# Engine orders held as tables in place of a list scheduler, in a fused attention and MLP kernel

## The chip, the cores and the metric

The kernel runs on one core of a Trainium2 chip. The metric is the device time of one execution in microseconds (us). Three runs of the kernel before gave a median of 744.11 us, from 744.04 to 744.46. The profile comes from one further execution.

## What is computed

The reference takes one batch of S = 2048 rows of D = 512 bfloat16 numbers. It normalises each row, and adds to the input an attention branch and an MLP branch that both read the normalised rows:

```python
def _A_ref(x, wq, wk, wv, wo):          # H = 32 heads of Dh = 16, one K and one V for all
    q = (x @ wq) by heads
    k, v = x @ wk, x @ wv
    scores = q k^T * Dh ** -0.5
    o = softmax(scores) @ v
    return o by rows @ wo
def _B_ref(x, w1, b1, w2, b2):          # F = 1792
    return gelu(x @ w1 + b1) @ w2 + b2
xn = _layernorm(x)
return x + _A_ref(xn, ...) + _B_ref(xn, ...)
```

## The kernel before

**Tiles.** The queries are cut into 4 blocks of 512 and the 32 heads into 8 groups of 4, which gives 32 pairs of block and group. For each pair the scores of 4 heads against 16 blocks of 128 keys are made as tiles of 128 keys by 512 queries: 64 tiles per pair, 2048 in all. Three tiles make a unit `u`; there are 683 units. Units use two sets of three PSUM banks in turn, so the scores of unit `u+2` overwrite those of unit `u`.

**A unit.** TensorE makes its three score tiles (L1055, one matmul each). A string in the code, `DTAB`, says which of the three go to VectorE; the others go to ScalarE. ScalarE takes the exponential of its one to three tiles in a single instruction (L1078, buffer `E`). For its tiles VectorE makes the exponential by integer arithmetic on the bits of a bfloat16: an add and clamp that reads PSUM and writes `Dt` (L1109, called the clamp below), and then, for a batch of tiles together, three steps that add constants and so make four shifted copies (L1156 on VectorE, called the posts; one of the three steps, an addition in place on one tile at a time, stands in L1152 and goes either to GpSimd or to VectorE). TensorE multiplies each `E` tile and each copy in `Dt` by a (scaled) V and adds them up in one PSUM bank, 32 of its 128 partitions for each of the four heads (L1122, called PV below). So an `E` tile costs one PV and a VectorE tile five.

**Side work.** Between these stand, on TensorE, the matmuls of the MLP and of the projections (L724, four at a time on 32 columns each, bank 7) and their evacuations on VectorE (L1221, L1249, L1301). At the end of each pair VectorE copies the sums out (L1168), DMAs re-lay them, and GpSimd or VectorE divides by the softmax sums (L1201). ScalarE computes the GELU of the MLP in two bursts, after units 182 and 512 (L1262). Some matmuls on zeros (L1419, L1420, L1422) fill gaps on TensorE.

**The end.** The last group's sums are normalised without DMAs: two shuffles on VectorE (L1209), for each half of 256 queries a logarithm (L1211) and an exponential (L1212) on ScalarE, two multiplies on VectorE (L1214); then the last output matmuls (`wol`, L724), three adds on VectorE (L1410), one copy on ScalarE (L1413), and the stores.

**What waits for what.** A score group waits until ScalarE and VectorE have read the banks that it overwrites: the exponential and the clamps of two units before. An exponential waits for its scores. A clamp waits for its scores and a free `Dt` slot; a PV waits for its exponential, post or GpSimd step. Every engine is given its own list of instructions and works through it in that order, so whatever stands in front of a waiting instruction decides when it is reached.

**What sets the order.** The kernel is recorded as a list of operations with reads and writes (`Prog.add`). Before emission a list scheduler (`Prog.schedule`, `Prog.pick_pe`) plays the program through with modelled durations: at each step it takes the engine that is free first, and of its ready operations the one with the earliest due time (ready time plus an allowance of its kind, or a number from the table `PRO_DUE` for the prologue). TensorE takes scores first; a clamp has an allowance of -20, so it goes ahead of posts (+1). A GpSimd step is started together with a VectorE instruction of at least 0.4 modelled us that is not `lock`ed (posts and some others are), and waits for a `gate`, the VectorE instruction before it. Where TensorE is expected idle the scheduler puts in matmuls on zeros. `Prog.emit` then turns dependences into semaphore waits and leaves out those that an earlier wait on the same engine already covers.

Of the kernel before, what the change touches and what calls it, by code (L numbers as in the profile page):

```python
# [10 lines left out]
P = 128  # L11
# [11 lines left out]
WIN = 3.413  # L23
HAM_T = 0.35
HAM_PHASE = 1.5

FILL_GAP = 0.25
FILL_U = 0.8
FILL_FROM = 30.0
PV_MIN = 2  # L30
PV_S = 1
P1_ALLOW = -20.0
EV_ALLOW = -2.0
S_WAIT = 0.1
P_WAIT = 0.0
# [3 lines left out]
PL_GATE = 0.1  # L39
PL_WIN = 0.4  # L40
PL_TAKE = 1.0
PL_DUE = 3.0
PL_START = 0.065
PL_SEM = 0.16
PL_FREE = 0.06
NE_ND_KB = (23, 19, 11, 6)
LA = 34
LB = 120
LY = 5
LP = 121  # L50
LS = 122
FIN_G = 2
FIN_F = 0
LAL = 30.0
LCO = 0.0
PRO_FROM = 2.0
GAP_BANK = 2
TBL = 1
# [5 lines left out]
Y_ALLOW = 2.0  # L64
H_ALLOW = 1.0
YT_ALLOW = (3,3,3,3)
WF_ALLOW = 1.5
QP_ALLOW = 1.5
# [11 lines left out]
EARLY = {23: 2}  # L80
FG = 7
UB2 = 2
YS = 19
HA = 58
HB = 168
Q_DUE = 16.0
# [14 lines left out]
PRO_DUE = (0,0,0,0,0,0,0,0,0,0,0,0.4,0.5,0.6,0.7,1017.1,901.894,890.936,0,911.47,982.75,1039.3,992.512,983.425,908.277,857.795,1021.4,984.567,1036.75,779.535,923.986,886.19,884.173,908.812,866.914,834.53,725.116,986.245,833.576,894.096,955.163,1016.7,841.68,1010.86,972.641,1071.46,918.455,991.63,996.77,917.66,1009.78,888.843,894.798,974.195,844.378,976.646,989.53,1004.34,861.884,890.838,860.34,962.694,933.585,834.453,733.954,908.291,843.106,1011.73,842.736,890.595,888.932,972.911,996.819,1013.78,960.534,901.05,840.158,948.36,842.524,854.02,1001.52,730.495,963.942,849.46,720.905,847.543,1027.14,854.874,859.03,995.253,996.641,1000.03,875.182,940.656,1013.08,927.264,901.825,865.47,856.153,1017.36,898.923,721.588,947.112,923.899,849.462,1031.22,1030.72,955.02,950.514,841.636,863.865,1004.42,992.309,974.33,882.517,1063.14,878.579,949.38,1005.69,1003.02,817.428,985.366,903.631,841.221,906.182,996.735,900.069,852.002,852.002,852.002,852.002,1009.23,962.572,984.69,1005.83,885.252,884.008,917.146,1057.84,908.105,1006.45,929.851,817.484,1057.79,1057.79,928.858,847.552,883.135,883.135,883.135,883.135,922.749,923.172,934.91,721.558,720.974,893.495,886.877,974.293,964.313,954.793,978.549,983.34,928.83,865.239,917.084,866.847,962.244,1027.57,864.398,920.685,923.146,941.861,844.389,901.982,1022.62,984.525,886.906,964.025,844.452,949.617,849.009,875.152,818.81,901.963,856.265,854.212,961.178,901.027,865.835,840.629,957.632,1025.29,1025.29,1025.29,1025.29,1025.29,1025.29,1025.29,949.479,1004.42,860.932,881.214,848.587,848.972,947.715,861.854,861.854,908.371,861.95,830.564,1013.59,920.851,852.231,848.667,834.623,834.623,873.394,849.031,984.612,984.612,983.72,865.867,901.395,857.833,1017.64,1052.68,991.698,950.486,1018.53,908.301,863.879,988.505,933.383,888.733,852.632,852.632,852.632,852.632,852.632,852.632,1001.37,972.862,921.214,1021.48,1021.48,1021.48,1021.48,1021.48,887.495,1015.8,875.099,1001.3,870.169,921.11,993.696,925.73,1005.52,961.579,848.728,1006.32,1008.12,876.619,942.093,990.844,990.844,990.844,990.844,994.103,987.859,1014.2,1014.2,1014.2,1012.8,1014.2,1014.2,1014.2,1014.2,860.884,855.696,855.696,844.754,855.696,855.252,855.696,895.571,985.973,1012.46,980.32,856.139,865.908,864.432,863.808,1004.31,985.998,788.801,903.822,865.794,984.664,894.041,1009.69,982.782,877.356,890.884,901.51,1027.88,899.618,997.552,997.552,963.952,935.705,935.705,962.628,989.577,926.43,865.864,863.945,853.609,967.557,837.03,1014.88,859.692,1006.82,1030.15,992.552,999.391,861.643,1009.24,857.784,829.305,826.367,None,None,None,None,None,920.941,None)  # L101
KV_ORD = (1, 2, 3, 4, 0)
KV_DVE = ()
DU = dict(sd=50.88, sa=19.13, ag=-17.19, ln=-33.66, xn=14.6, xa=-30.73, tr=-23.53, eva=22.21, evd=14.86, k=23.66, kt=26.82, km=39.07, v=-7.76, q=15.28, vf=17.24, v0=29.19, qt0=9.89)
# [8 lines left out]

class _Op:
    __slots__ = ("eng", "fn", "deps", "sdeps", "stream", "amt", "need", "ticket", "waits", "clock", "occ", "lat",
                 "allow", "kind", "tag", "nun", "outs", "rel", "lock", "pm", "rdy", "start", "end", "vis", "idx", "done", "due", "real", "docc")


class Prog:
# [5 lines left out]
    def __init__(self, nc):  # L125
        self.nc = nc
        self.ops = []
        self.writer = {}
        self.readers = {}
        self.accs = {}  # L130
        self.chain = {}
        self.in_chain = True
        self.filler = None
        self.pro_filler = None
        self.fill_gap = None
        self.fill_deps = []
        self.early = []
        self.log = []

    def add(self, eng, fn, r=(), w=(), acc=None, dma=None, occ=0.1, lat=0.15, allow=1.0, kind=None, tag=None, after=(), due=None, lock=False, docc=0.0):  # L140
        if len(self.ops) < len(PRO_DUE):
            due = PRO_DUE[len(self.ops)]
# [7 lines left out]
        op.occ, op.lat, op.allow, op.kind, op.tag = occ, lat, allow, kind, tag  # L150
        op.idx = len(self.ops)
        op.done = False
        op.due = due
        op.rel = None
        op.pm = any(k == ("bank", 7) or k[0] == ("bank", 7) for k in w)
        deps, sdeps = {}, {}

        def dep(o, raw):
            if o is None or o is op:
                return  # L160
            if o.stream == eng == "pe":
                sdeps.setdefault(id(o), (o, False))
                return
            deps[id(o)] = o
            sdeps[id(o)] = (o, True)
# [26 lines left out]
        for o in after:  # L192
            sdeps.setdefault(id(o), (o, True))
        if self.in_chain:
            o = self.chain.get(eng)
            if o is not None:
                sdeps.setdefault(id(o), (o, False))
            self.chain[eng] = op
        op.sdeps = list(sdeps.values())
# [3 lines left out]
    @staticmethod  # L203
    def due(o):
        return (o.rdy + o.allow if o.due is None else o.due), o.idx

    def pick_pe(self, t, cand, allr, mode, visit, cgbusy):
        S = [o for o in cand if o.kind == "S"]
        rest = [o for o in cand if o.kind != "S"]
        nxt = min([o.rdy for o in allr if o.kind == "S"] + [t + 9.0])  # L210
        if mode == "col":
            end = max(cgbusy)
            if t < end - 0.01:
                if t < end - 0.216 + 0.03:
                    c = [o for o in rest if o.tag is not None and cgbusy[o.tag[1]] <= t]
# [12 lines left out]
        if S:  # L228
            return S[0]
# [1231 lines left out]
```

## Time and profile before

| | before |
|---|---|
| median of 3 runs | 744.11 us (744.04 to 744.46) |
| the profiled execution: its own time | 744.43 us |
| its span, first to last instruction | 742.7 us |
| TensorE matmul busy (modelled ends) | 727.6 us, 9030 matmuls |
| VectorE busy | 730.4 us, 1411 instructions |
| ScalarE busy | 730.9 us, 744 instructions |
| GpSimd busy | 382.9 us, 548 instructions |
| granted TensorE clock | 1.00 |

Between the span and the time of that execution lie 1.73 us outside the first and last instruction, and that execution was 0.32 us over the median. In the page, PE is TensorE's matmuls, PEld its weight loads, DVE VectorE, ACT ScalarE, POOL GpSimd, SP the queue that issues DMAs. Busy is the union of an engine's recorded instructions; records of neighbours can overlap, since an instruction is recorded as started while the one before it still drains. Idle before an instruction is put down to whoever released it last.

### The profile page before, as it was taken

To read this page: it belongs to the slowest core of one execution; us is meant where nothing else is said; L and a number is where in the kernel's file an instruction comes from. 1 tells how busy PE (TensorE), PEld (TensorE's weight loads), DVE (VectorE), ACT (ScalarE), POOL (GpSimd) and SP (SyncE) were. 2 spreads that over 40 slices of the span, in tenths; PEclk is the share of its full clock that TensorE was granted. 3 is DMA by queue.
4 is the path that set the end of the run, shared out by engine and by line. 5 is a ranking of instruction groups with operands and counts; after the bars stand their busy time and mean duration, and the time that the engine had idled before them with its cause. 6 is when DMAs were issued, how large, how long until landed. Compare 5 with 4: busy or idle time off the path is not lost.

```text
span 742.7 us, 22080 instructions
## 1 busy us (share of the span) xinstructions
PE 727.6 (98%) x9030; PEld 212.4 (29%) x9030; DVE 730.4 (98%) x1411; ACT 730.9 (98%) x744; POOL 382.9 (52%) x548
## 2 busy tenths in 40 slices
PE   7999999999999999999999999999998999999998
PEld 4322222222233222222222222222232222222222
DVE  8999999999999999999999999999999999999996
ACT  8899999999999999999999999999999999999997
POOL 7444555554533546545656455343644656555561
PEclk9999999999999999999999999999999999999999
DMA  9200100000010010100101010100100101010011
GB/s 304 74 19 17 30 11 17 24 11 16 15 46 24 18 37 18 24 16 14 27 13 28 25 39 16 35 20 11 23 17 23 29 20 38 16 37 26 10 30 38
DMA packets 31198, 23.34 MB, mean 31 GB/s; under 512 B 16385, under 2 KB 25722, under 8 KB 31098
## 3 DMA queue, kind: packets, MB, share of 16 engines
q1 hardware_dynamic: 30954, 21.80, 11.1%
q8 instruction: 72, 1.18, 0.7%
q14 instruction: 28, 0.23, 0.1%
q10 hardware_dynamic: 144, 0.13, 0.1%
HBM read 13.08 MB, written 2.35 MB: 21 GB/s over the span
## 4 chain that ended last, share of the span: by engine, by line
ACT 70%; PE 19%; DVE 8%; DMA 1%; SPq 1%; issue 0%; DVEq 0%
ACT E L1078 70%; PE pAll L1122 8%; PE pAll L1055 6%; PE pAll L724 4%; DVE Dt L1109 4%; DVE Dt L1156 3%; DMA b1row<-in_B_b_dram 1%; SPq L731 1%; DVE Of L1168 0%; PE pAll L718 0%; PE pAll L1422 0%; DVE x_sb L1249 0%; DVE xnT L877 0%; DVE ub L1410 0%; DVE qp L1221 0%
## 5 line engine op out<-in xcount | busy, mean ns | idle before, releaser
L1078 ACT ACTIVATE E<-pAll 128x1024 bf16<-128x1024 f32 (+1 forms) x676 | 680.5, 1282 | 0.7 <-PE pAll L1055 0.5
L1152 POOL TENSOR_SCALAR Dt<-Dt 128x512 int16<-128x512 int16 x454 | 342.2, 754 | 325.5 <-DVE Dt L1156 112.6
L1122 PE MATMUL pAll<-Dt,V 128*32 128x512 bf16 x2775 | 408.2, 383 | 2.4 <-DVE Dt L1156 1.3
L1109 DVE TENSOR_SCALAR Dt<-pAll 128x512 int16<-128x512 f32 (+1 forms) x541 | 369.8, 698 | 1.4 <-PE pAll L1055 0.3
L1122 PE MATMUL pAll<-E,V 128*32 128x512 bf16 x1493 | 303.6, 383 | 0.2 <-DVE Of L1168 0.2
L1156 DVE TENSOR_SCALAR Dt<-Dt 128x1024 int16<-128x1024 int16 (+6 forms) x540 | 290.1, 564 | 0.4
L1055 PE MATMUL pAll<-QT,KT 32*128 32x512 bf16 x2048 | 267.1, 384 | 4.6 <-ACT E L1078 2.4
L1055 PEld LDWEIGHTS pAll<-QT,KT 32*128 32x128 bf16 x2048 | 66.6, 90 | 295.4 <-ACT E L1078 282.3
L1122 PEld LDWEIGHTS pAll<-Dt,V 128*32 128x32 bf16 x2775 | 102.6, 95 | 102.7 <-issue 68.0
L1122 PEld LDWEIGHTS pAll<-E,V 128*32 128x32 bf16 x1493 | 72.7, 94 | 44.0 <-issue 33.1
L724 PE MATMUL pAll<-xnT,w_sb 128*32 128x512 bf16 x896 | 84.8, 383 | 0.0
L724 PE MATMUL pAll<-w_sb,x_sb 128*32 128x512 bf16 x448 | 76.6, 384 | 0.0
L724 PE MATMUL pAll<-w_sb,ub 128*32 128x512 bf16 x448 | 64.3, 383 | 0.1
L724 PE MATMUL pAll<-wop,oTp 128*32 128x512 bf16 x256 | 51.2, 382 | 0.0
L1201 POOL TENSOR_TENSOR oTp<-OfP,rbP 128x256 bf16<-128x256 f32 (+1 forms) x28 | 22.5, 809 | 14.5 <-DVE Dt L1156 7.9
L724 PEld LDWEIGHTS pAll<-xnT,w_sb 128*32 128x32 bf16 x896 | 21.4, 95 | 26.7 <-issue 16.8
L724 PE MATMUL pAll<-xnT,wq_sb 128*32 128x512 bf16 x256 | 26.8, 383 | 0.0
L1152 DVE TENSOR_SCALAR Dt<-Dt 128x512 int16<-128x512 int16 x101 | 26.6, 286 | 0.0
L1168 DVE COPY Of<-pAll 128x512 f32<-128x512 f32 x31 | 21.2, 685 | 0.1
L1249 DVE TENSOR_SCALAR x_sb<-pAll,b1T 128x512 bf16<-128x512 f32 x28 | 20.8, 744 | 0.0
L1249 DVE TENSOR_SCALAR ub<-pAll,b1T 128x512 bf16<-128x512 f32 x28 | 20.8, 743 | 0.0
L724 PEld LDWEIGHTS pAll<-w_sb,x_sb 128*32 128x32 bf16 x448 | 18.4, 95 | 8.1 <-issue 6.6
(121 smaller groups left out, 260.8 us busy)
## 6 DMA issues: line engine op xcount, KB each, us to landing
OfP<-Of SPq DMA_DIRECT2D x124, 32.0 KB, 2.0
rbP<-rden_rows SPq DMA_DIRECT2D x124, 32.0 KB, 1.8
w_sb<-in_B_w_dram SPq DMA_DIRECT2D x2, 1792.0 KB, 11.3
x_sb<-in_A_x_dram SPq DMA_DIRECT2D x18, 128.0 KB, 2.3
QT<-qp SPq DMA_DIRECT2D x124, 16.0 KB, 1.8
x_sb<-in_A_x_dram SPq DMA_DIRECT2D x7, 256.0 KB, 4.4
out_dram<-x_sb SPq DMA_DIRECT2D x12, 128.0 KB, 1.9
wq_sb<-in_A_wq_dram SPq DMA_DIRECT2D x1, 512.0 KB, 5.8
```

Source lines behind the costliest of these rows:

```text
L724: add("pe", lambda e, c=c, j=j: e.matmul(o[c, :], l[:, c], rh, start=start, stop=stop, tile_position=(0, 32 * j)), r, [(k, j) for k in w] ...
L731: return add(eng, lambda e: e.dma_start(o, i), r, w, dma=stream, occ=occ, lat=lat, allow=allow, **kw)
L1055: ins = e.matmul(o, l, rh, start=True, stop=True, tile_position=(q0, 0))
L1078: o = act(lambda e: e.activation(E[:, s0:s0 + na, :], bank(b0, na).rearrange("p (a n) -> p a n", a=na), ACT.Exp, scale=LN2 / 128.0), w=[B( ...
L1109: op = dve(lambda e: e.tensor_scalar(Dt[:, s:s + n, :], bank(bk, n).rearrange("p (a n) -> p a n", a=n), float(127 * 128) + SPL_D, SPL_MIN, ...
L1122: add("pe", lambda e, a, b: e.matmul(pO[32 * j:32 * j + 32, :], V1[:, v, kt, :], rhs, start=a, stop=b, tile_position=(0, 32 * j)), r=r + [ ...
L1152: add("pool", lambda e, d=d, k=k: e.tensor_scalar(d, d, 1.0, float(k), ALU.mult, ALU.add), [], [(("D", base[o > 0] + q), o)], occ=PL_OCC, ...
L1156: dve(lambda e, d=view(o, nb), q=view(i, nb), k=k: e.tensor_scalar(d, q, float(k), None, ALU.add), r=keys(i), w=keys(o), n=nb * n * TBW, m ...
L1168: op = dve(lambda e: e.tensor_copy(Of[:, i, :], pO), w=["O", ("Of", i)], allow=0.0)
L1201: "pool", lambda e, c=c: e.tensor_tensor(oTp[0:n, sl, c], OfP[0:n, s, c], rbP[0:n, s, c], ALU.mult),
L1249: dve(lambda e: e.tensor_scalar(ubs[tb % 2][:, ft, :], pM, b1T[:, ft:ft + 1], None, ALU.add), r=["b1T"], w=M4 + [ukey(tb, ft)], n=TBW + 57 ...
```

## The change

The scheduler with its allowances, `PRO_DUE` and the rules for fillers is taken out. In its place stand tables: `ORD`, for each engine a string of two-character numbers that says how far each operation moves from its place in the recorded list; `GATE`, for each GpSimd step either that VectorE does it, or which operation it waits for besides its data, or none; and `FILLS`, the places and waits of the 154 matmuls on zeros. `Prog.arrange` reads them. The operations, their engines (101 of the L1152 steps stay on VectorE), the tiles, buffers, `DTAB` and `Prog.emit` stay as they were, so the same instructions run; only their order on an engine, the gates of GpSimd, and with them which semaphore waits are left, can differ.

```diff
-    def pick_pe(self, t, cand, allr, mode, visit, cgbusy):
...
-    def schedule(self):
...
+FILLS = ((0, 'p', 0, (18, 28)),
...
+         (5800, 'O', 2, (18,)),
+         (5804, 'O', 0, (18,)))
...
+def numbers(s):
+    n = len(ABC)
+    at = {c: i for i, c in enumerate(ABC)}
+    return [at[a] * n + at[b] - n * n // 2 for a, b in zip(s[::2], s[1::2])]
...
+    def arrange(self):
         ops = self.ops
+        for o, g in zip([o for o in ops if o.kind == "pl"], numbers(GATE), strict=True):
+            if g == ON_DVE:
+                o.eng = o.stream = "dve"
+                o.kind, o.occ, o.lat = "post", o.docc, D_LAT
+            elif g:
+                o.deps.append(ops[o.idx + g])
+                ops[o.idx + g].need = True
+        seq = {}
+        for e, _ in self.SECTIONS:
+            own = [o for o in ops if o.eng == e]
+            seq[e] = [own[i + d] for i, d in enumerate(numbers(ORD[e]))]
+            assert len({o.idx for o in seq[e]}) == len(own) == len(seq[e])
+        for p, kind, cg, ids in FILLS:
...
+            seq["pe"].insert(p, f)
...
+        while any(at[e] < len(seq[e]) for e in seq):
+            n = len(out)
+            for e in seq:
+                while at[e] < len(seq[e]) and all(id(o) in done for o in seq[e][at[e]].deps):
+                    out.append(seq[e][at[e]])
+                    done.add(id(out[-1]))
+                    at[e] += 1
+            assert len(out) > n
...
-        pr.schedule()
+        pr.arrange()
```

What the tables do to the orders, engine by engine: SyncE's 508 entries stand as before, so every DMA is issued in the old order. On ScalarE two neighbours of 733 change places. On VectorE 1409 entries stand in both orders, and 1003 of them can be kept in one common sequence; on GpSimd 400 of 544; on TensorE 2391 of 7511 (fillers left out). Up to the first score groups, at 23.5 us of the trace, all five engines have the old order with the old waits.

**Place 1: VectorE, the stretch that ran from 75.6 to 80.4 us.** L1109 (after: L936) are clamps, L1156 (L982) posts, L1249 (L1073) the evacuation of an MLP matmul, L1182 (L1006) a reciprocal of softmax sums. Before:

```order
L1156 TENSOR_SCALAR Dt<-Dt 128x2x1536
L1109 TENSOR_SCALAR Dt<-pAll 128x512 x2
L1249 TENSOR_SCALAR ub<-pAll,b1T 128x512
L1109 TENSOR_SCALAR Dt<-pAll 128x512
L1182 RECIPROCAL den<-den 128x32
L1156 TENSOR_SCALAR Dt<-Dt 128x1536
L1156 TENSOR_SCALAR Dt<-Dt 128x512
L1109 TENSOR_SCALAR Dt<-pAll 128x512
```

After, the same place:

```order
L982 TENSOR_SCALAR Dt<-Dt 128x2x1536
L936 TENSOR_SCALAR Dt<-pAll 128x512 x2
L1073 TENSOR_SCALAR ub<-pAll,b1T 128x512
L982 TENSOR_SCALAR Dt<-Dt 128x1536
L1006 RECIPROCAL den<-den 128x32
L936 TENSOR_SCALAR Dt<-pAll 128x512
L982 TENSOR_SCALAR Dt<-Dt 128x512
L982 TENSOR_SCALAR Dt<-Dt 128x2x1536
```

The clamp after the evacuation has moved behind the post of 1536 columns and the reciprocal. Place 1 is one of many of this kind: 241 clamps have more VectorE work ahead of them than before, 72 less, 228 the same.

**Place 2: TensorE after the second GELU burst, the stretch that ran from 566.5 to 571.4 us.** L1055 (L884) are score groups, L1122 (L949) PVs, L1422 (L1234) matmuls on zeros, L718 (L554) sums of squares of the queries. Before:

```order
L1422 MATMUL pAll<-xnT,zeros 32x512 x4
L1122 MATMUL pAll<-Dt,V 32x512 x19
L1055 MATMUL pAll<-QT,KT 128x512 x3
L718 MATMUL pAll<-sqq,sel 32x512
L1122 MATMUL pAll<-E,V 32x512
L718 MATMUL pAll<-sqq,sel 32x512
L1122 MATMUL pAll<-Dt,V 32x512 x3
L1122 MATMUL pAll<-E,V 32x512
L1122 MATMUL pAll<-Dt,V 32x512 x3
L1055 MATMUL pAll<-QT,KT 128x512 x3
```

After:

```order
L949 MATMUL pAll<-Dt,V 32x512 x2
L554 MATMUL pAll<-sqq,sel 32x512
L1234 MATMUL pAll<-xnT,zeros 32x512
L949 MATMUL pAll<-Dt,V 32x512 x5
L884 MATMUL pAll<-QT,KT 128x512 x3
L949 MATMUL pAll<-Dt,V 32x512
L949 MATMUL pAll<-E,V 32x512
L949 MATMUL pAll<-Dt,V 32x512 x5
L884 MATMUL pAll<-QT,KT 128x512 x3
```

Both sums of squares now stand ahead of the first score group shown. The run of 19 PVs in front of that group is broken up: among those that have moved behind it are the PVs of the two latest posts that the run waited for, and the later of these two posts has itself moved behind six instructions that followed it on VectorE, two clamps among them.

**Place 3: the end of ScalarE's program.** L1078 (L906) is the last exponential of the scores, L1211 (L1035) the logarithm and L1212 (L1036) the exponential of the last normalisation, one instruction for each half of the queries. Before:

```order
L1078 ACTIVATE E<-pAll 128x1536
L1078 ACTIVATE E<-pAll 128x1024
L1211 ACTIVATE rbP<-rbP 128x256 x2
L1212 ACTIVATE rbP<-rbP,lnb 128x256 x2
L1413 ACTIVATE ub<-pAll 128x512
```

After:

```order
L906 ACTIVATE E<-pAll 128x1536
L906 ACTIVATE E<-pAll 128x1024
L1035 ACTIVATE rbP<-rbP 128x256
L1036 ACTIVATE rbP<-rbP,lnb 128x256
L1035 ACTIVATE rbP<-rbP 128x256
L1036 ACTIVATE rbP<-rbP,lnb 128x256
L1228 ACTIVATE ub<-pAll 128x512
```

The first half's exponential has moved ahead of the second half's logarithm; nothing else moves on ScalarE.

More of the change, by code (lines that the diff above doesn't have):

```diff
@@ L111, in vcost @@
     return n / 0.96e3 / mode + 0.065
+def numbers(s):
+    n = len(ABC)
+    at = {c: i for i, c in enumerate(ABC)}
+    return [at[a] * n + at[b] - n * n // 2 for a, b in zip(s[::2], s[1::2])]
 class _Op:
-    __slots__ = ("eng", "fn", "deps", "sdeps", "stream", "amt", "need", "ticket", "waits", "clock", "occ", "lat",
-                 "allow", "kind", "tag", "nun", "outs", "rel", "lock", "pm", "rdy", "start", "end", "vis", "idx", "done", "due", "real", "docc")
+    __slots__ = ("eng", "fn", "deps", "odeps", "stream", "amt", "need", "ticket", "waits", "clock", "occ", "lat", "kind", "tag", "lock", "idx", "real", "docc")
 class Prog:
@@ L130, in __init__, with add @@
         self.accs = {}
[L131 to L142, printed above, removed]
+        self.fillers = {}
+    def add(self, eng, fn, r=(), w=(), acc=None, dma=None, occ=0.1, lat=0.15, kind=None, tag=None, lock=False, docc=0.0):
         op = _Op()
@@ L149, in add @@
         op.ticket = None
-        op.occ, op.lat, op.allow, op.kind, op.tag = occ, lat, allow, kind, tag
+        op.occ, op.lat, op.kind, op.tag = occ, lat, kind, tag
         op.idx = len(self.ops)
[L152 to L156, printed above, removed]
+        deps, odeps = {}, {}
         def dep(o, raw):
@@ L191, in add @@
             self.accs.setdefault(acc, []).append(op)
[L192 to L199, printed above, removed]
+        op.odeps = list(odeps.values())
         self.ops.append(op)
         return op
-    @staticmethod
-    def due(o):
-        return (o.rdy + o.allow if o.due is None else o.due), o.idx
@@ L1056, in fn @@
                 return ins
-            return add("pe", fn, r, [B(3 * x + i) for i in range(len(ts))], occ=0.216, lat=S_LAT, allow=-1.0, kind="S")
+            return add("pe", fn, r, [B(3 * x + i) for i in range(len(ts))], occ=0.216, lat=S_LAT, kind="S")
         eptr = [0]
@@ L1110, in p1 @@
                                                  float(127 * 128) + SPL_D, SPL_MIN, ALU.add, ALU.max),
[L1111 removed]
+                       w=[B(b) for _, b in ds] + [(("D", s + i), 0) for i in range(n)], n=n * TBW, kind="p1")
             for i, (t, _) in enumerate(ds):
```

661 lines of the change are left out of this document (160 added, 501 removed), and 151 rows, old and new, of the table FILLS.

## The prediction

> **What bounds the kernel now.** I looked first at the span, then at busy time by stretch, then at what each group of instructions waited for, and last at the tail.
>
> ```profile
> span 742.7 us, 22080 instructions
> ```
>
> The view of busy time by stretch, for ScalarE alone, from the first exponential of the scores to the last:
>
> ```profile
> 24.00:200.00 176.00, 176.00 (x174) 1.00 0.08 18
> 200.00:240.00 40.00, 39.63 (x32) 1.00 0.12 31
> 240.00:540.00 300.00, 300.00 (x299) 1.00 0.10 23
> 540.00:580.00 40.00, 39.70 (x32) 1.00 0.09 21
> 580.00:735.00 155.00, 155.00 (x156) 1.00 0.10 25
> ```
>
> The columns are the stretch, its length, ScalarE's busy time with its instructions, the granted clock, and DMA. In these 711 us ScalarE is idle for 0.37 + 0.30 = 0.67 us, all of it in the two stretches with the GELU bursts. The same view for VectorE:
>
> ```profile
> 40.00:200.00 160.00, 159.55 (x296) 1.00 0.08 18
> 200.00:400.00 200.00, 199.51 (x375) 1.00 0.10 24
> 400.00:600.00 200.00, 199.62 (x388) 1.00 0.10 25
> 600.00:700.00 100.00, 99.77 (x196) 1.00 0.09 22
> ```
>
> VectorE is idle for 0.45, 0.49, 0.38 and 0.23, 1.55 us in these 660. So both engines are full. Which of them paces the other shows first in the costliest group (count, then busy us and mean ns of one, then idle before):
>
> ```profile
> L1078 ACT ACTIVATE E<-pAll 128x1024 bf16<-128x1024 f32 (+1 forms) x676 | 680.5, 1282 | 0.7 <-PE pAll L1055 0.5
> ```
>
> The 676 exponentials wait 0.7 us in all. Their records add up to 676 x 1.282 = 866.6 us and cover 680.5, so each overlaps the next by 0.28 on the mean; an exponential is issued that much before the one ahead of it has drained. And in the list of waits the score groups name who released them:
>
> ```profile
> PEld pAll L1055 <- ACT E L1078: 282.3, 652, 0.8
> PEld pAll L1055 <- DVE Dt L1109: 9.4, 21, 0.7
> ```
>
> 652 score groups waited for an exponential to leave their banks, 21 for a clamp. So ScalarE paces the loop: an exponential ends, the scores run, ScalarE is still in the next exponential, and VectorE's clamp has nearly always been done in time. The exponentials are the same and in the same order after the change, so this stage can gain at most 0.67 us, and a new order can lose whatever ScalarE is made to wait.
>
> **What the change can't move.** Up to the first score group order and waits are as before, so the first exponential starts just before 24 us again. The DMAs keep their order on their one queue; those of the tail are taken with it.
>
> **Part 1: the waits after the GELU bursts go, in part.** The timeline of TensorE and then of ScalarE at these places:
>
> ```profile
> 568.20 1.76 PE L1122 MATMUL pAll<-Dt,V 128*32 128x512 bf16 x19 [1.06 <-DVE Dt L1156]
> ...
> 569.89 0.39 PE L1055 MATMUL pAll<-QT,KT 32*128 32x512 bf16 x3
> ...
> 226.61 0.39 PE L1055 MATMUL pAll<-QT,KT 32*128 32x512 bf16 x3
> ...
> 227.05 1.45 ACT L1078 ACTIVATE E<-pAll 128x1536 bf16<-128x1536 f32 x1 [0.32 <-PE pAll L1055]
> ```
>
> Before the score group of 569.89 (place 2 of the change) TensorE idles 1.06 us for a post, then works off 19 PVs, and ScalarE's 0.30 us in that stretch follow. In the new order the PVs of the two latest posts and both sums of squares no longer stand between; I count the 0.30 as gone. At 227.05 the exponential waited 0.32 for scores that stood behind side matmuls. The new order puts more of these ahead of the score group that ends the burst (117 against 85) and fewer ahead of the next (35 against 60), while ScalarE is still in GELU; whether 0.32 goes I can't tell, and take half. Bounds: 0 and 0.67. Value: -0.30 - 0.16 = -0.46 us.
>
> **Part 2: clamps moved behind posts.** This is the side that can lose, and place 1 shows its size. VectorE and then ScalarE there:
>
> ```profile
> 77.69 0.75 DVE L1249 TENSOR_SCALAR ub<-pAll,b1T 128x512 bf16<-128x512 f32 x1
> 78.34 0.69 DVE L1109 TENSOR_SCALAR Dt<-pAll 128x512 int16<-128x512 f32 x1
> 78.94 0.35 DVE L1182 RECIPROCAL den<-den 128x32 f32<-128x32 f32 x1
> 79.20 0.70 DVE L1156 TENSOR_SCALAR Dt<-Dt 128x1536 int16<-128x1536 int16 x2
> ...
> 77.86 2.60 ACT L1078 ACTIVATE E<-pAll 128x1024 bf16<-128x1024 f32 x2
> ...
> 78.76 1.70 ACT L1078 ACTIVATE E<-pAll 128x1536 bf16<-128x1536 f32 x1
> ```
>
> The clamp of 78.34 ended at 79.03. Moved behind the reciprocal (start to next start 79.20 - 78.94 = 0.26) and the post of 1536 columns (mean record 0.55, less the 0.09 by which VectorE's records here overlap the next: 78.34 + 0.69 - 78.94; 0.46), it ends at 79.03 + 0.26 + 0.46 = 79.75. That 0.55 is from this group:
>
> ```profile
> L1156 DVE TENSOR_SCALAR Dt<-Dt 128x1536 int16<-128x1536 int16 x49 | 27.0, 551 | 0.1
> ```
>
> The scores that overwrite its bank then take 0.39 (the row of 569.89), so with some 0.1 for the two hand-overs (the exponential of 227.05 started 0.05 after the scores of 226.61 had ended) their exponential is fed at 80.24. ScalarE is in the exponential of 78.76 until 80.46, and would take the next one in about 0.28 before, at 80.18. So the moved clamp costs some 0.06 us at the most here, and no more because the exponential in between is one of three tiles.
>
> I did this sum for every score group that has a clamp before it, 534 of them: durations by shape from the trace, clamps shifted by the work put before them. In the old order each has spare time, 0.08 us at the least; in the new one three have none, by 0.05 us at most, and a few PVs that stand before scores near 80 to 110 us come out 0.1 us late. Once ScalarE is 0.1 late, later groups have 0.1 more, so such delays don't add up. Bounds: 0 (VectorE has 1.55 us of idle time to run ahead in) and 1.37, the largest shift of a clamp in this sum, 1.45, less the smallest spare time of the old order, 0.08, as if they met. Value: +0.15, nearest to place 1, where some 0.06 is lost.
>
> **Part 3: VectorE's and GpSimd's own time.** The instructions are the same. What stands directly behind one that it must wait for (a step on the result of the instruction before) are 18 cases against 15 in the old order; each costs VectorE the drain of about 0.09, the overlap above, 0.3 us in all, less than the 1.55 us of idle time: 0. GpSimd is half idle:
>
> ```profile
> L1152 POOL TENSOR_SCALAR Dt<-Dt 128x512 int16<-128x512 int16 x454 | 342.2, 754 | 325.5 <-DVE Dt L1156 112.6 <-PE pAll L1122 77.0 <-DVE Dt L1109 58.8
> ...
> 224.57 0.62 POOL L1152 TENSOR_SCALAR Dt<-Dt 128x512 int16<-128x512 int16 x1
> ```
>
> Its steps take 0.62 us when nothing is in the way and 0.754 on the mean, so 454 x 0.134 = 61 us are spent beside something else, hidden in its idle 325.5. What is hidden there costs nothing; the PVs that wait for it are counted in part 2.
>
> **Part 4: the tail.** From the end of the last exponential (733.80 + 1.32 = 735.12) to the end of the span are 7.58 us:
>
> ```profile
> 733.80 1.32 ACT L1078 ACTIVATE E<-pAll 128x1024 bf16<-128x1024 f32 x1
> 736.13 0.91 ACT L1211 ACTIVATE rbP<-rbP 128x256 f32<-128x256 f32 x2 [1.01 <-DVE rbP L1209]
> 736.94 0.89 ACT L1212 ACTIVATE rbP<-rbP,lnb 128x256 f32<-128x256 f32 x2
> ...
> 737.47 0.90 DVE L1214 TENSOR_TENSOR oT<-pAll,rbP 128x256 bf16<-128x256 f32 x2 [0.88 <-ACT rbP L1212]
> 738.48 1.89 DVE L1410 TENSOR_TENSOR ub<-pAll,ub 128x512 bf16<-128x512 f32 x3
> ```
>
> With place 3 the first half's exponential starts when its logarithm is done, about 736.6 in place of 736.94, so the first multiply starts about 0.35 earlier. The second multiply needs four ScalarE steps as before and ends near 738.37 as before (737.47 + 0.90). The three adds follow it on VectorE; they started 0.11 after it, for the output matmuls, which the earlier first half now brings forward. So 0.1 of the 0.35 arrives at the end, and the stores are issued that much earlier. Bounds: +0.2 (three more matmuls, 68 against 65, stand behind the last PV, four at a time: one more group of about 0.2) and -0.35. Value: -0.1.
>
> **The sum.** Against the profiled execution's own time: 744.43 - 0.46 + 0.15 + 0 - 0.1 = 744.02 us. That execution lay 0.32 over the median of the runs, so for a median: 743.7. The difference from 744.11 is 0.06%; about 0.2%, 1.5 us, is what a measurement of this kernel can tell from no change.
>
> **Rivals.** *The spare time is spent* (0.20): parts 1 and 4 give nothing and part 2 takes its bound: 744.11 + 1.37 = 745.5. For it speaks that the new order takes the spare time at many score groups; against it, that place 1 falls on a long exponential, and that the delays don't add up. It would still be within 0.2%, just.
>
> *VectorE gets slower* (0.14), the way to a slower kernel. In the groups with shapes kept apart VectorE's steps on `Dt` show no stretching: 110 posts of 512 columns take 285 ns on the mean, the 101 L1152 steps of the same size on VectorE 286, with no idle time before them:
>
> ```profile
> L1156 DVE TENSOR_SCALAR Dt<-Dt 128x512 int16<-128x512 int16 x110 | 29.9, 285 | 0.0
> L1152 DVE TENSOR_SCALAR Dt<-Dt 128x512 int16<-128x512 int16 x101 | 26.6, 286 | 0.0
> ```
>
> So it is GpSimd that stretches (0.754 against 0.62), and VectorE that goes first. The old scheduler saw to that: it let a GpSimd step begin with a long unlocked VectorE instruction. The new table has 141 GpSimd steps with no wait of their own, against 77, and more posts in a row. If a post then meets a GpSimd step that is under way, it may wait for up to the 0.62 of it, 0.3 on the mean, and everything behind it on VectorE, clamps included, is that much later. It decides from the point where this exceeds VectorE's 1.55 us of idle time and the gains of 0.6 and 1.5 more, that is 3.7 us or 12 such meetings; with 16 (4.8 us) the kernel takes 744.11 + 4.8 - 1.55 - 0.56 = 746.8. The Trainium skill bears on this (SBUF — State Buffer, "Who interferes with whom"): it says that VectorE in its two-port modes and GpSimd take turns on a shared pair of ports, and that whoever issues first holds it for the whole instruction. The trace agrees in that GpSimd's 0.62 became 0.754; that VectorE is ever the one that is held no row here shows. By that rule alone, with issue order left to chance, the sum would come out on this rival's side; the gates and the data waits left in the new table speak against that.
>
> *More than counted* (0.06): all 0.67 us go, the tail gives its 0.35, and half a microsecond more comes from stores or exponentials closer together: 744.11 - 0.67 - 0.35 - 0.5 = 742.6. No row shows a place for the last half.
>
> That the tables only restate the old order is excluded by the places shown.
>
> **Chances.** The forecast 0.60, the spent time 0.20, VectorE 0.14, more than counted 0.06. The range runs from 742.9 (743.7 less the rest of part 1, 0.21, of part 4, 0.25, of part 2, 0.15, and half the 0.42 by which the runs before differ) to 745.9, over the 745.5 of the spent time and into the first of the VectorE case; it leaves out less than 0.2. Within 0.2% are the first two cases, 0.80; slower 0.14, faster 0.06.
>
> **What would show it.** Right: in the profile after, ScalarE idle under 0.4 us from 24 to 735, no wait of 1 us before the PVs near 568, the last exponential ending within 0.5 us of 735.12, and the first L1214 multiply about 0.35 earlier after it. The score groups that wait for a clamp should be more than 21, without ScalarE idling for them. Part 2 is wrong if ScalarE idles by more than a few tenths between 50 and 110 us; part 3 is wrong if the mean of a 512-column post rises over 285 ns or clamps stretch. The forecast is wrong if the median is under 742.6 or over 745.6.

## The result and the profile after

The changed kernel takes 764.36 us (median of 6 runs, 763.82 to 764.95), the kernel before 744.20 in 6 runs beside them (744.02 to 744.63). The ratio is 1.027, with a 95% interval of 1.0257 to 1.0283. So the change costs 20.2 us, and the forecast of 743.7, with a range up to 745.9, was wrong. The span of the profiled execution:

```profile
span 762.3 us, 22088 instructions
```

Busy time by stretch for ScalarE, with the columns as before:

```profile
24.00:200.00 176.00, 174.37 (x170) 1.00 0.08 17
200.00:240.00 40.00, 39.80 (x31) 1.00 0.11 30
240.00:540.00 300.00, 296.11 (x291) 1.00 0.10 22
540.00:580.00 40.00, 39.43 (x31) 1.00 0.07 16
580.00:755.00 175.00, 170.22 (x169) 1.00 0.10 25
```

and for VectorE:

```profile
40.00:200.00 160.00, 159.62 (x289) 1.00 0.08 18
200.00:400.00 200.00, 199.36 (x367) 1.00 0.09 23
400.00:600.00 200.00, 199.80 (x371) 1.00 0.11 24
600.00:700.00 100.00, 100.00 (x197) 1.00 0.11 26
```

ScalarE is now idle for 11.07 us in 731, in every stretch (0.9 of it after the last exponential), and VectorE for 1.22 in 660, less than before. It has no more idle time to give and is later all the same, so it does its work more slowly. Which work, the groups tell: first the posts of the kernel before (its 101 in-place steps took 26.6 us, by the row shown in the prediction), then the posts and the in-place steps of the changed kernel.

```profile
L1156 DVE TENSOR_SCALAR Dt<-Dt 128x1024 int16<-128x1024 int16 (+6 forms) x540 | 290.1, 564 | 0.4
```

```profile
L982 DVE TENSOR_SCALAR Dt<-Dt 128x1024 int16<-128x1024 int16 (+6 forms) x540 | 305.8, 594 | 0.5
L978 DVE TENSOR_SCALAR Dt<-Dt 128x512 int16<-128x512 int16 x101 | 29.8, 304 | 0.0
```

The same 540 posts take 305.8 us in place of 290.1, and the 101 in-place steps 29.8 in place of 26.6: 18.9 us more, nearly the whole loss, and none of it is idle time. With the shapes kept apart, the posts of 512 and of 1536 columns that the prediction showed:

```profile
L982 DVE TENSOR_SCALAR Dt<-Dt 128x512 int16<-128x512 int16 x110 | 36.6, 339 | 0.1
...
L982 DVE TENSOR_SCALAR Dt<-Dt 128x1536 int16<-128x1536 int16 x49 | 29.1, 594 | 0.1
```

They go from 285 to 339 ns and from 551 to 594. Clamps are not slower (the 534 single ones 677 ns, before 684). GpSimd's own steps take what they took, 757 ns on the mean against 754:

```profile
L978 POOL TENSOR_SCALAR Dt<-Dt 128x512 int16<-128x512 int16 x454 | 343.8, 757 | 351.3 <-PE pAll L949 165.7 <-DVE Dt L982 78.8 <-DVE Dt L936 34.6
```

**One place in both traces.** VectorE around the evacuation at 435.88 us of the kernel before, and then GpSimd:

```profile
435.88 0.73 DVE L1249 TENSOR_SCALAR ub<-pAll,b1T 128x512 bf16<-128x512 f32 x1
436.54 0.68 DVE L1156 TENSOR_SCALAR Dt<-Dt 128x2048 int16<-128x2048 int16 x1
437.13 0.68 DVE L1109 TENSOR_SCALAR Dt<-pAll 128x512 int16<-128x512 f32 x1
437.74 0.41 DVE L1156 TENSOR_SCALAR Dt<-Dt 128x1024 int16<-128x1024 int16 x1
...
436.70 0.99 POOL L1152 TENSOR_SCALAR Dt<-Dt 128x512 int16<-128x512 int16 x1 [0.17 <-DVE ub L1249]
```

The GpSimd step is released by the evacuation (its gate) and starts while the post of 436.54 is running. Its record is 0.99 us long, where an undisturbed one is 0.62, so it stands behind that post for 0.37. It then runs beside the clamp and is done at 437.69, just ahead of the next post. The same step after, released by the same evacuation:

```profile
445.66 0.75 DVE L1073 TENSOR_SCALAR ub<-pAll,b1T 128x512 bf16<-128x512 f32 x1
446.33 0.42 DVE L982 TENSOR_SCALAR Dt<-Dt 128x1024 int16<-128x1024 int16 x1
446.66 0.71 DVE L978 TENSOR_SCALAR Dt<-Dt 128x512 int16<-128x512 int16 x1
447.29 0.67 DVE L936 TENSOR_SCALAR Dt<-pAll 128x512 int16<-128x512 f32 x1
...
446.49 0.73 POOL L978 TENSOR_SCALAR Dt<-Dt 128x512 int16<-128x512 int16 x1 [0.28 <-DVE ub L1073]
```

Behind the first post now stands not a clamp but another step on `Dt`. GpSimd gets in between the two, and the second, 0.28 us elsewhere, takes 0.71. Its record shows no wait: a held instruction counts as busy.

**The gates.** The table `GATE` names, for each of the 440 GpSimd steps that wait for more than their data, the very VectorE instruction that the scheduler had chosen; not one gate is another. What changed is VectorE's work behind it. Before, behind 409 of the 440 stands one locked instruction (a post, mostly) and then an unlocked one (a clamp, an evacuation), as in the first fence. After, that is so behind 187; behind 107 stand two locked ones, and behind 146 an unlocked one at once. Of the 66 posts and in-place steps that are held in the changed kernel (the experiments say what counts as held), 28 are held by a step of the 107, 23 by one of the 146, 13 by one of the 187, and two by a step without such a gate.

### The profile page after: what moved, and what is told of

Its sections match the earlier page's. It is cut to its first block, busy times and chain, and to the rows that moved or that the text cites. A ratio compares the mean times of both kernels' runs of the same rounds, so it can differ in the third digit from the quotient of the medians.

```text
span 762.3 us, 22088 instructions
## 1 busy us (share of the span) xinstructions
PE 736.6 (97%) x9030; PEld 221.0 (29%) x9030; DVE 750.9 (99%) x1411; ACT 740.5 (97%) x744; POOL 386.6 (51%) x548
## 4 chain that ended last, share of the span: by engine, by line
PE 51%; DVE 45%; issue 2%; ACT 1%; DMA 1%; SPq 0%; DVEq 0%
PE pAll L949 22%; DVE Dt L936 19%; DVE Dt L982 16%; PE pAll L884 16%; PE pAll L559 12%; DVE Of L994 1%; DVE Dt L978 1%; DVE ub L1073 1%; DVE x_sb L1073 1%; DVE qp L1045 1%; DVE stats L663 1%; PE pAll L1234 1%; DMA x_sb<-in_A_x_dram 1%; DVE ub L693 1%; PE pAll L554 0%
## 5 line engine op out<-in xcount | busy, mean ns | idle before, releaser
L906 ACT ACTIVATE E<-pAll 128x1024 bf16<-128x1024 f32 (+1 forms) x676 | 690.0, 1146 | 10.2 <-PE pAll L884 6.9
L949 PE MATMUL pAll<-Dt,V 128*32 128x512 bf16 x2775 | 439.6, 384 | 1.6 <-DVE Dt L982 0.7
L936 DVE TENSOR_SCALAR Dt<-pAll 128x512 int16<-128x512 f32 (+1 forms) x541 | 363.5, 691 | 0.3 <-PE pAll L884 0.2
L949 PE MATMUL pAll<-E,V 128*32 128x512 bf16 x1493 | 335.4, 384 | 0.6 <-DVE Of L994 0.4
L982 DVE TENSOR_SCALAR Dt<-Dt 128x1024 int16<-128x1024 int16 (+6 forms) x540 | 305.8, 594 | 0.5
L884 PE MATMUL pAll<-QT,KT 32*128 32x512 bf16 x2048 | 267.1, 384 | 14.7 <-DVE Dt L936 11.5
L884 PEld LDWEIGHTS pAll<-QT,KT 32*128 32x128 bf16 x2048 | 68.5, 90 | 295.9 <-ACT E L906 210.4
L949 PEld LDWEIGHTS pAll<-Dt,V 128*32 128x32 bf16 x2775 | 109.4, 94 | 97.8 <-issue 58.9
L559 PE MATMUL pAll<-xnT,w_sb 128*32 128x512 bf16 x896 | 122.8, 383 | 1.2 <-DVE ub L1073 0.3
L949 PEld LDWEIGHTS pAll<-E,V 128*32 128x32 bf16 x1493 | 80.9, 94 | 44.7 <-issue 31.1
L559 PE MATMUL pAll<-xnT,wq_sb 128*32 128x512 bf16 x256 | 41.1, 383 | 0.0
L559 PEld LDWEIGHTS pAll<-xnT,w_sb 128*32 128x32 bf16 x896 | 30.6, 94 | 32.0 <-issue 16.8
L1234 PE MATMUL pAll<-xnT,zeros 128*32 128x512 bf16 x124 | 30.1, 383 | 0.0
L978 DVE TENSOR_SCALAR Dt<-Dt 128x512 int16<-128x512 int16 x101 | 29.8, 304 | 0.0
L1025 POOL TENSOR_TENSOR oTp<-OfP,rbP 128x256 bf16<-128x256 f32 (+1 forms) x28 | 24.4, 877 | 6.0 <-DVE Dt L982 3.3
L559 PEld LDWEIGHTS pAll<-w_sb,ub 128*32 128x32 bf16 x448 | 17.5, 95 | 14.7 <-issue 9.7
```

The lines of the kernel that those rows point to most:

```text
L559: add("pe", lambda e, c=c, j=j: e.matmul(o[c, :], l[:, c], rh, start=start, stop=stop, tile_position=(0, 32 * j)), r, [(k, j) for k in w] ...
L884: ins = e.matmul(o, l, rh, start=True, stop=True, tile_position=(q0, 0))
L906: o = act(lambda e: e.activation(E[:, s0:s0 + na, :], bank(b0, na).rearrange("p (a n) -> p a n", a=na), ACT.Exp, scale=LN2 / 128.0), w=[B( ...
L936: op = dve(lambda e: e.tensor_scalar(Dt[:, s:s + n, :], bank(bk, n).rearrange("p (a n) -> p a n", a=n), float(127 * 128) + SPL_D, SPL_MIN, ...
L949: add("pe", lambda e, a, b: e.matmul(pO[32 * j:32 * j + 32, :], V1[:, v, kt, :], rhs, start=a, stop=b, tile_position=(0, 32 * j)), r=r + [ ...
L978: add("pool", lambda e, d=d, k=k: e.tensor_scalar(d, d, 1.0, float(k), ALU.mult, ALU.add), [], [(("D", base[o > 0] + q), o)], occ=PL_OCC, ...
```

## The experiments

**Theories.** *Theory 1*: a GpSimd step that is under way holds the next post, and the kernel is slower by what posts lose so. *Theory 2*: TensorE's new order makes scores late. *Theory 3*: the clamps that moved behind posts make scores wait, whatever GpSimd does.

In the table, a post or in-place step on VectorE is "met" if a GpSimd record that began before VectorE's preceding instruction ended runs for 20 ns or more past that end (where the post itself starts later than that end, its own start is taken); its loss is the time from end to end, less the median of the unmet ones of the same shape in the kernel before. It is "held" if it loses more than 0.05 us; the lost time is that of all met ones. GpSimd's 28 divides count like its steps; 3 of the 66 in the changed kernel are held by one. A few met ones wait for the result of the clamp or post ahead as well (5 in the changed kernel, 0.6 us). The last column is TensorE's wait for GpSimd ahead of PVs.

| kernel | median, us | met | held | lost, us | PVs wait, us |
|---|---|---|---|---|---|
| before | 744.20 | 18 | 8 | 1.1 | 4.5 |
| changed | 764.36 | 184 | 66 | 22.6 | 5.1 |
| new_refit | 748.03 | 51 | 24 | 4.1 | 5.8 |
| old_no_gates | 769.89 | 263 | 104 | 31.8 | 1.1 |
| new_short_steps | 744.82 | 77 | 5 | 1.7 | 1.6 |
| old_short_steps | 744.36 | 1 | 1 | 0.2 | 1.8 |
| old_late_gates | 753.50 | 220 | 127 | 16.8 | 7.5 |
| new_other_memory | 765.10 | 179 | 71 | 23.7 | 5.1 |
| new_half_steps | 805.18 | 351 | 252 | 43.1 | 45.1 |
| new_refit_2 | 757.59 | 28 | 14 | 3.1 | 21.9 |
| new_refit_2_undone | 757.26 | 38 | 20 | 5.6 | 17.8 |
| new_refit_2_queue | 752.81 | 40 | 19 | 5.0 | 11.9 |

### new_refit: the new orders, other gates

```diff
-GATE = "Q]Q[QZQ~QnPz##PtPsQoR*R)QiPz##PqQDQZQ:
+GATE = "Q#Q#Q#Q#QnQ###Q#Q#QAR5Q?Q#P2##QjQ9QaQ[
...
```

For each step the first place in the changed kernel's trace was sought, from when its data is there, where it fits beside unlocked VectorE work; its gate is the instruction ahead of the last locked one before that place. That moves 369 gates; 88 of these steps wait for their data alone afterwards. Of the 367 gates that are left, 351 have again one locked instruction and then an unlocked one behind them.

> The changed kernel with all five engine orders as they are, and only the gates of 369 GpSimd steps moved to other VectorE instructions, so that a step begins while the last post ahead of a clamp or an evacuation is still running. Theory 1 (a GpSimd step that is under way holds back the next post, and 184 such meetings cost VectorE some 21 us): the meetings fall to under 40, VectorE's posts of 512 columns go from 339 back to 285 to 300 ns, and the time is 744 to 749 us. Theory 2 (TensorE's new order makes the scores late) and theory 3 (clamps stand behind posts on VectorE, whatever GpSimd does): no order moved, so 760 to 765 us.

Measured: 748.03 us, ratio 1.0052 (1.0035 to 1.0068). With all five orders left as they are, 16.3 of the 20.2 us are gone, as theory 1 has it. The meetings fall to 51, more than the 40 that were expected at most, and the posts of 512 columns to

```profile
L982 DVE TENSOR_SCALAR Dt<-Dt 128x512 int16<-128x512 int16 x110 | 31.1, 290 | 0.1
```

### old_no_gates: the old orders, no gates

```diff
-GATE = "Q]Q[QZQ~QnPz##PtPsQoR*R)QiPz##PqQDQZQ:
+GATE = "Q#Q#Q#Q#Q#Q###Q#Q#Q#Q#Q#Q#Q###Q#Q#Q#Q#
...
```

(`Q#` is the number 0. The orders are the old ones as tables; the kernel before has no `GATE`, so the line with the minus is the changed kernel's, which names the same gates.)

> The kernel before, all orders as they are, with the 440 gates of GpSimd taken out; a step waits for its data alone. Theory 1: many steps start while posts stand next on VectorE, over 100 meetings at some 0.12 us each, so 755 to 775 us. Theories 2 and 3: no order moved and waits only taken out, so 742 to 745 us.

Measured: 769.89 us, ratio 1.0345 (1.0329 to 1.036). Waits were only taken away, no order was touched, and the result is slower than the changed kernel. The posts:

```profile
L982 DVE TENSOR_SCALAR Dt<-Dt 128x512 int16<-128x512 int16 x110 | 34.2, 323 | 0.0
```

So the gates were worth 25.5 us before, and a loss of this size needs neither theory 2 nor theory 3.

### new_short_steps and old_short_steps: what the orders cost by themselves

```diff
-add("pool", lambda e, d=d, k=k: e.tensor_scalar(d, d, 1.0, float(k), ALU.mult, ALU.add),
+add("pool", lambda e, d=d, k=k: e.tensor_scalar(*[d if e is nc.vector else d[:, 0:8]] * 2, 1.0, float(k), ALU.mult, ALU.add),
```

> The changed kernel, orders and gates as they are; the 454 additions in place that GpSimd does on 512 columns are done on 8 columns only, so that the other 504 keep their old values (this part of the computation is left out). Theory 1: a step that is met is over in under 0.15 us, so posts lose nearly nothing: 742 to 747 us. Theories 2 and 3: GpSimd is not what is waited for, so 757 to 765 us.

> The kernel before, orders and gates as they are, with the same 454 additions cut to 8 columns (that part of the computation is left out). The control for the run with short steps in the changed kernel. All theories: ScalarE paces as before, so 742 to 745 us; what the changed kernel with short steps lies above this is what theories 2 and 3 together can claim.

Measured: 744.82 us in the changed kernel (ratio 1.0006, 0.9996 to 1.0015) and 744.36 in the kernel before (1.0001, 0.9991 to 1.001). With the steps short, the new orders and the old ones can't be told apart. (A step on 8 columns took 197 ns at its shortest, more than the 0.15 us of the expectation; the posts lost nearly nothing all the same.) Yet the score groups of the changed kernel still wait for clamps, as they do with full steps:

```profile
PEld pAll L884 <- DVE Dt L936: 35.2, 76, 1.1
```

In the changed kernel itself the row reads

```profile
PEld pAll L884 <- DVE Dt L936: 38.3, 77, 1.1
```

The 77 groups are 56 more than before, as the prediction had foreseen, and cost next to nothing while VectorE is not held. Theories 2 and 3 together are left with 0.46 us at the most, less than can be measured; in part even this is posts held by divides, which the edit leaves as they were (1.7 us lost in the table, against 0.2).

### old_late_gates: one instruction later

```diff
-GATE = "Q]Q[QZQ~QnPz##PtPsQoR*R)QiPz##PqQDQZQ:
+GATE = "Q4Q3Q2QhQWQ###Q#Q#P#Q@Q?QzQ###QhQ,QDQ[
...
```

The gate of 409 steps is moved from the instruction ahead of a post to the post itself (the line with the minus is again the changed kernel's, with the same gates as before).

> The kernel before, all orders as they are, with 409 of its 440 gates moved one VectorE instruction later: from the instruction ahead of the post to the post itself, so that a GpSimd step is released when the post has ended and no more while it runs. Theory 1 (a step under way holds the next post): each step starts some 0.1 to 0.2 us later beside its clamp of 0.6 us and reaches that much into the post behind it; with 150 to 250 meetings at 0.05 to 0.15 us this is 752 to 770 us. The rival, that only the rough place of the steps matters and not a tenth of a microsecond: 743 to 746 us.

Measured: 753.5 us, ratio 1.012 (1.0105 to 1.0135), with 220 meetings, inside what theory 1 expected. A step that is released at the end of the post, and no longer while it runs, reaches past its clamp into the next post. 71 of the 211 posts and in-place steps of 512 columns are met; 45 of these lose 45 to 51 ns, 16 lose 144 to 185. Over all shapes such small pieces add up to the 16.8 us of the table, and the kernel is 9.1 us slower. On GpSimd the same change looks like a gain:

```profile
L978 POOL TENSOR_SCALAR Dt<-Dt 128x512 int16<-128x512 int16 x454 | 284.9, 628 | 392.3 <-DVE Dt L982 202.5 <-PE pAll L949 115.0 <-PE pAll L559 25.1
```

Its steps take 628 ns in place of 754. So the 0.134 us that each step seemed to lose before was the step standing in line behind a post, as the scheduler's gates had arranged it.

### new_other_memory: is it `Dt`, or the way to it?

```diff
+scr2 = sb([P, TBW], i16, "scr2")
...
-e.tensor_scalar(d, d, 1.0, float(k), ALU.mult, ALU.add)
+e.tensor_scalar(*((d, d) if e is nc.vector else (scr2[:], xnT[:, 0, 0:TBW].bitcast(i16))), 1.0, float(k), ALU.mult, ALU.add)
```

> The changed kernel, orders and gates as they are; the 454 GpSimd steps read 512 columns of xnT and write 512 columns of a buffer of their own, in place of adding in Dt (that addition is left out), and each waits for the end of the one before it. Theory 1 in its port form (the two engines share a way to SBUF, whatever they touch): the posts are held as before, 760 to 767 us. Its rival, that they meet over the same tile of Dt or that a post waits for the step's result: 743 to 750 us.

Measured: 765.1 us, ratio 1.0274 (1.0259 to 1.0289), with 179 meetings and 23.7 us. The posts are held just the same while GpSimd touches other buffers. So it is not the tile. Nor is it a result that is waited for; that this run can't show, as its semaphores are the same, but the program does: of the waits that `Prog.emit` leaves in either kernel, none makes a post or in-place step on VectorE wait for GpSimd (three clamps do).

### new_half_steps: two steps of 256 columns

```diff
-e.tensor_scalar(d, d, 1.0, float(k), ALU.mult, ALU.add)
+[e.tensor_scalar(c, c, 1.0, float(k), ALU.mult, ALU.add) for c in ([d] if e is nc.vector else [d[:, 0:256], d[:, 256:512]])][-1]
```

> The changed kernel, orders and gates as they are, with each of the 454 GpSimd steps on 512 columns cut into two on 256 columns, so that the same sum is done in two instructions. If a step holds the port to the end of its own instruction and lets a waiting post in between: a met step holds a post for half as long, while there are more meetings, so 750 to 762 us. If the port is shared finer than by instructions: the same bytes and more overhead, 763 to 772 us.

Measured: 805.18 us, ratio 1.0815 (1.0799 to 1.0831), outside both expectations. A step on 256 columns takes 0.404 us at its shortest against 0.619 for 512 in the changed kernel, so the same addition takes 0.81 us in place of 0.62. There are 351 meetings, and now PVs wait for GpSimd:

```profile
PEld pAll L949 <- POOL Dt L978: 45.1, 73, 2.2
```

What was wrong in the expectation is the number of meetings and this wait. The single hold did halve. Of the posts and in-place steps of 512 columns that are met, one in ten takes longer than this from end to end (unmet ones take 201 ns):

| GpSimd step, columns | 8 (new_short_steps) | 256 (new_half_steps) | 512 (changed) |
|---|---|---|---|
| its shortest record, ns | 197 | 404 | 619 |
| met post, 9th decile, ns | 227 | 411 | 624 |
| held, ns | 26 | 210 | 423 |

A hold grows by about 0.8 ns per column (423 - 210 over 256) and is 0.17 to 0.20 us shorter than the step's record.

### new_refit_2, and two partial returns: gates that come too late

```diff
-Q#TvUHR0RNQ#PoRTQFQnQDQ#Q#OxOw
+Q#TvUHR0ReQ#PoRTQFQzQDQ^Q#OxOw
...
```

(A piece of `GATE`; so are the next two.)

> The changed kernel with its orders and the refitted gates, refitted once more from the trace of that run: 79 gates moved again, with 0.70 us per step in place of 0.62, as two steps do not fit beside two clamps. The first refit left 51 meetings and 4.05 us. Theory 1: meetings under 35 and under 2.5 us, 744.5 to 747.5 us. Theories 2 and 3, which can claim no more than the 0.5 us by which the short steps differ: the same number; above 748.5 us theory 1 lacks something.

Measured: 757.59 us, ratio 1.0171 (1.0154 to 1.0188). The meetings fell to 28, as expected, what is lost in them to 3.1 us, not under 2.5, and the kernel is 9.6 us slower than with the first refit. By the words of the expectation theory 1 lacks something here: something else took the place of the meetings. TensorE shows it near 545 us:

```profile
543.83 0.39 PE L884 MATMUL pAll<-QT,KT 32*128 32x512 bf16 x3
545.14 0.60 PE L949 MATMUL pAll<-Dt,V 128*32 128x512 bf16 x5 [0.92 <-POOL Dt L978]
...
545.90 0.39 PE L884 MATMUL pAll<-QT,KT 32*128 32x512 bf16 x3
```

The PVs wait 0.92 us for a GpSimd step whose gate had moved to a later instruction, and the score group of 545.90 stands behind them. The same wait in the list of waits, second refit:

```profile
PEld pAll L949 <- POOL Dt L978: 21.9, 42, 1.4
```

In the first refit it was 5.8 us in 22 waits. To test this, moved gates were put back in part:

```diff
-Q#QmQ_Q#Q8Q#R#Q#Q#QSQ#
+Q#QmQ_Q#Q#Q#R#Q#Q#QSQ#
...
```

> The second refit with 17 of its 79 moved gates put back to where the first refit had them: those whose GpSimd step was read by a PV less than 0.3 us after its end. The second refit had fewer meetings than the first (28 against 51) and was still 9.6 us slower; TensorE's PVs waited 21.9 us for GpSimd steps in it, against 5.8. If that is the cause (a gate that comes too late feeds PVs late, and the scores stand behind them): the PVs' wait falls under 9 us and the time to 745 to 750 us. If something else in the 79 moves is: 754 to 758 us.

Measured: 757.26 us (1.0153 to 1.0187), which is where the other branch, something else in the 79 moves, had put it. But the wait itself hardly fell, to 17.8 us in place of under 9, so the 17 gates did not do what the test needed. A reading made after this run: GpSimd works in order, so a late gate also holds the steps queued behind it.

```diff
-R0QvT1WMQZQmQPQ#QmQ_Q#Q8
+R0QvT1VyQZQmQPQ#QmPkQ#Q8
...
```

> The second refit with 32 of its 79 moved gates put back to where the first refit had them: in its trace 28 PVs started right after the GpSimd step that they read, and the 32 are the moved gates of those steps and of the steps queued just ahead of them on GpSimd (12 of the 17 of the last run are among them; that run left out the ones queued ahead). If late gates, by way of GpSimd's queue, feed PVs late: the PVs' wait for GpSimd falls from 21.9 to under 10 us and the time to 745 to 751 us. If the waits have another origin: 754 us or more, and the cause of the second refit's loss stays open.

Measured: 752.81 us (1.0097 to 1.0131). The wait fell to 11.9 us, not quite to what was expected, and the time by half of the 9.6 us, to between the two branches. Over the four refits wait and time go together (5.8, 11.9, 17.8, 21.9 us and 748.0, 752.8, 757.3, 757.6). That late steps feed PVs late is shown at the place above and fits the four; that they are the whole 9.6 us is not shown. None of these versions beats the kernel before.

## Why the prediction was wrong

**The step that failed is part 3**, "The instructions are the same. (...) less than the 1.55 us of idle time: 0." The posts and in-place steps took 18.9 us more, by 66 held in place of 8. It took durations from the old trace as properties of the instructions, when they were properties of the order: a post of 512 columns took 285 ns because in the old order hardly ever a GpSimd step was under way when it was its turn (3 of 211 were met, against 67). The sentence behind it, that what GpSimd loses is hidden, read the 0.134 us per step rightly as standing in line, but not who had arranged it.

**The rival "VectorE gets slower"** named the mechanism, its place and the row that would show it (a 512-column post over 285 ns), and missed the size: 746.8 for 764.4.
- The price came out right, in part by luck: 66 held posts and in-place steps lost 22.0 us, 0.33 each, where 0.3 was taken. But 0.3 was half of a step's 0.62, for any meeting. Over all 184 meetings the mean is 0.12, since the other 118 lose 0.5 us together; and half of the 66 lose 0.42 or more.
- The number was wrong: 58 more held than before, where 16 were priced. The evidence taken was the number of steps without a wait of their own, 141 against 77. What counts is what stands behind each gate on VectorE, and that could be read from the two orders beforehand: 409 of 440 gates followed by a locked and then an unlocked instruction, against 187 after. That "the gates and the data waits left in the new table speak against that" was the error itself: they were left, and left where they no longer fit.
- The spare time of 1.55 us was probably too small. Counted from the end of the instruction before, the 534 single clamps of the kernel before took 5.5 us more than if each had taken 598 ns, the lower quartile in old_short_steps; in the changed kernel this is 1.6, without gates 0.3 and with late gates 0.1. Read as time that VectorE could give, most of it inside records, it turns the 30.7 us more lost in old_no_gates into 25.5, which is what was measured, and the 15.7 in old_late_gates into 10.3, measured 9.1. It does not account for new_refit: 2.9 us more lost, less 3.1 given, is about nothing, and 3.7 were measured. So this reading is rough, and what is left of the loss in new_refit is open.

By the same reading, the sum in the changed kernel is 22.6 - 1.1 = 21.5 us of losses, less 3.9 that its clamps had to spare (5.5 against 1.6), 17.6; the tail adds 0.6 (8.2 from the last exponential's end at 754.10 to the end of the span, 7.6 before), and some 2 us are not assigned.

**The Trainium skill** (SBUF — State Buffer, "Who interferes with whom") says that the second engine to issue on the shared pair is fully blocked, and that issue order decides who that is. The traces agree that the order decides, with the same instructions: before it was nearly always GpSimd that was held (754 ns on the mean against 617 at the shortest, and 8 held posts), after it is VectorE as well (757 ns against 619, and 66 held posts). How much of a record the page means by "for the whole instruction" these runs can't tell: in the changed kernel a 512-column step held a post for about 0.42 us, 0.45 in the longest case, of the 0.62 of its record. The prediction had cited this rule and said that by it alone the sum would come out on the rival's side. The weight that it gave to the gates against it was the mistake.

**Parts 1, 2 and 4** can be read from the two kernels with short steps. ScalarE in the two stretches with the GELU bursts, new orders first, then old:

```profile
200.00:240.00 40.00, 39.94 (x32) 1.00 0.13 32
...
540.00:580.00 40.00, 39.88 (x33) 1.00 0.08 20
```

```profile
200.00:240.00 40.00, 39.63 (x31) 1.00 0.12 31
...
540.00:580.00 40.00, 39.69 (x32) 1.00 0.08 20
```

*Part 1* gained 0.50 us (0.18 idle against 0.68), where -0.46 was forecast. *Part 2*: from the first exponential's start to the last one's end the new orders take 711.58 us, the old 711.17, so besides the 0.50 won some 0.9 was lost, in place of 0.15 and within the bounds of 0 and 1.37. A part of it, 0.35, is one wait of ScalarE at 674.5 us, and its cause is not the one that part 2 names. VectorE, GpSimd and ScalarE there, new orders with short steps:

```profile
672.38 1.17 DVE L982 TENSOR_SCALAR Dt<-Dt 128x512 int16<-128x512 int16 x2
...
672.54 0.73 POOL L1025 TENSOR_TENSOR oTp<-OfP,rbP 128x256 bf16<-128x256 f32 x1 [0.63 <-DVE Dt L936]
...
674.85 1.02 ACT L906 ACTIVATE E<-pAll 128x1024 bf16<-128x1024 f32 x1 [0.35 <-PE pAll L884]
```

A divide (L1025) gets in between two posts and holds the second, of 1024 columns, for 0.56 us; the clamps behind it, the scores and the exponential follow late. The rest of the 0.9 left no gap on ScalarE, and its place is not shown. *Part 4*, in the changed kernel itself: the first multiply starts 0.99 us after the first logarithm (755.58, then 756.57), before 1.34, and the adds start 0.17 earlier; of this 0.1 was forecast at the end, and with short steps nothing arrives there (6.69 us from the first logarithm to the end of the span against 6.59). Rows of the tail of the changed kernel, ScalarE and then VectorE:

```profile
755.58 0.42 ACT L1035 ACTIVATE rbP<-rbP 128x256 f32<-128x256 f32 x1 [1.48 <-DVE rbP L1033]
...
756.57 0.42 DVE L1038 TENSOR_TENSOR oT<-pAll,rbP 128x256 bf16<-128x256 f32 x1 [0.53 <-ACT rbP L1036]
...
757.76 1.94 DVE L1225 TENSOR_TENSOR ub<-pAll,ub 128x512 bf16<-128x512 f32 x3
```

So the forecast of no measurable change held for the orders by themselves (1.0006 with short steps), if with some luck in the parts: -0.50, +0.9 and +0.1 in place of -0.46, +0.15 and -0.1. It failed for the orders together with gates that had been fitted to others. That ScalarE paces was true before and false after: in the page's chain of work that ended last, ScalarE has 70% of the span before and 1% after, VectorE 8% and 45%, TensorE 19% and 51%. The sign that the prediction named for it, ScalarE's idle time, shows only half of the loss: the exponentials wait 10.2 us of the 19.0 by which the last one ends later,

```profile
L906 ACT ACTIVATE E<-pAll 128x1024 bf16<-128x1024 f32 (+1 forms) x676 | 690.0, 1146 | 10.2 <-PE pAll L884 6.9 <-PE pAll L949 0.3
```

and their mean record is shorter than before (1146 ns against 1282) in a slower kernel, as they overlap less: the 676 add up to 774.7 us and cover 690.0, before 866.6 and 680.5.

## What to carry to other kernels

Where GpSimd works beside VectorE steps like these posts, the duration of each in a trace belongs to the order it was taken in. Count, for each GpSimd step, what stands on VectorE behind the instruction that releases it, before trusting that duration in a new order. A release that queues the step behind a running post and beside a clamp hid it almost whole (8 held posts); the same release one instruction later cost 9 us here, no gate at all 26, and one that comes too late for the matmul that needs the step makes TensorE wait instead (0.92 us at the place shown). When an order is changed, gates and other waits that encode the old neighbours have to be derived again with it.

## What the hardware showed that was not expected

A GpSimd step on 512 columns held a 512-column post for 0.42 us of its 0.62 in the ninth decile, one on 256 columns for 0.21 of 0.40, and one on 8 columns for 0.03 of 0.20: the hold followed the columns, about 0.8 ns each, and was 0.17 to 0.20 us shorter than the step's record. Cutting a step in two halved the hold and added 0.19 us to the same addition; more posts were held (252 for 66), PVs came to wait, and the kernel became 41 us slower. Clamps, which read PSUM, show no hold: in the changed kernel 318 of them began while GpSimd was in an instruction and took 598 ns from end to end in the median (601 on the mean), the 216 others 599 (602). And a held instruction is recorded as busy, not as waiting (the 0.71 us at 446.66), so the list of waits shows nothing of it.
